# A fused retention and MLP kernel on one core: 64-token attention chunks and a rearranged lead-in

## The chip, the cores and the metric

The kernel runs on one core of a Trainium2 chip. The metric is the device time of one execution in microseconds (us), as a median over the fast runs. PE is the TensorE (matmul) engine, PEld its weight loads, DVE the VectorE, ACT the ScalarE, POOL the GpSimd engine, SP the SyncE. In this kernel POOL and SP issue the DMA transfers. Instants in a trace are us from the start of the profiled span, which is some 1.8 us shorter than the time reported for the run.

## The reference

It is a retention attention (causal, with one decay factor for each head) followed by an MLP with a sigmoid-approximated gelu.

```
# q, k, v: (8, 8, 576, 64) float32
scores = matmul(q, k.T) / sqrt(64)
D[h, i, j] = gamma[h] ** (i - j) if i >= j else 0
x = matmul(scores * D, v)            # to (8 * 576 = 4608, 512) tokens
h = x @ w_in                         # 512 x 2048
out = (h * sigmoid(1.702 * h)) @ w_out   # 2048 x 512, float32
```

## The kernel before

The 4,608 tokens are 36 units of 128 tokens; four units are a chunk of 512 tokens, and there are nine chunks, 0 to 8. For a chunk PE makes the up projection (16 groups of four 128x512 matmuls, each group followed by a gelu on ACT) and the down projection (four units of 16 matmuls). The attention of the next chunk's units is put into the down projection as two "blocks" of two units each. A unit needs its q, k and v loaded, q and k transposed (on PE for units 0 to 7, by DMA from unit 8 on), v scaled, scores, a running state of k and v for the tokens of earlier units, and the values.

The parts that the change touches, with cuts marked:

```
def lead_in():
    load_kq(0, 0); load_kq(0, 1)      # k and q of unit 0, POOL's (software) queue, cast to bf16
    load_v(0, eng="sp")
    load(1); load_win(0); load(2); load(3)
    for i in range(1, 4): load_win(i)
    for i in range(4): load_wout(i)
    for u in range(4, 10): load(u)    # ten units in all
    ...
def state(u):                         # 4 matmuls 128x128x128, of which half the result is used
    for hp in range(4): ... bank["K"] += k_pair.T @ v_pair
    ...                               # two casts on DVE to kv[u]
def block(j):                         # units 2j and 2j+1
    inter(2*j, 0); inter(2*j+1, 1)    # kv of the earlier units times q
    first = values_half(...)          # half of scores @ v
    scores(u, b) for the next two units
    values_half(..., phase 1)
    x_out_pair(...)
def steady():
    if c == 1:
        for u in range(10, 14): load(u, after=["T1_0"])      # wait for the transpose of unit 9
    for u in range(4*c + 6, 4*c + 10): dma_transpose(u)
    for u in range(4*c + 10, 4*c + 14): load(u, after=[transpose of unit 4*c + 9])
    ...                               # up groups, with state(m) after f = 2, 6, 10, 14
    ...                               # down groups, block after the first of units 0 and 2
```

`after=` makes a load wait for a DMA transpose. The names T0 to T7 are the eight buffers of transposed q and k; unit u uses T(u mod 8).

## Time and profile before

The kernel took 304.84 us (median of 3 runs, 304.63 to 305.48).

| what | us |
|---|---|
| first up group starts (timeline of PE) | 16.66 |
| down projection of chunk 0 starts | 35.76 |
| chunk 1 starts | 56.53 |
| chunk 1 takes | 31.68 |
| chunks 2 to 7 take | 183.95 |
| chunk 8, to PE's end | 27.83 |

The chain of waits of the same kernel around the change from chunk 0 to chunk 1, its longest pieces only (start, duration, engine, what, line; an x is a number of instructions):

```profile
52.05 1.73 PE psB L583 x8
...
54.29 0.76 DVE xT L550 x2
55.05 1.21 DVE pm L503 x2
...
56.60 0.76 PE psA L572 x4
...
74.33 2.54 PE psA L583 x11
76.86 3.45 PE psB L583 x16
```

Line 572 is the up projection, line 583 the down projection. In this stretch no DMA stands in the chain: the transposes of units 10 to 13 come in time.

A block as the timeline of PE shows it; the down group that is interrupted ends at about 195.6 and goes on at 196.9:

```profile
194.66 1.03 PE L583 MATMUL psA<-w_out_sb,gT 128*128 128x512 bf16 x4
195.62 0.24 PE L468 MATMUL psX<-kqT,kv 64*64 64x128 bf16 x1
...
196.89 2.54 PE L583 MATMUL psA<-w_out_sb,gT 128*128 128x512 bf16 x11 [0.16 <-issue]
```

### The profile page before, as it was taken

Reading aid. Unit: us, or ns where it says so; the run is one execution under the profiler, and the core shown is the slowest. Engines: PE = TensorE matmul, PEld = TensorE weight load, DVE = VectorE, ACT = ScalarE, POOL = GpSimd, SP = SyncE. Lnnn points to the kernel's source line nnn. Section 1 sums busy time; section 2 is a strip of 40 time slices with the busy share of each in tenths; the row PEclk is TensorE's granted clock in tenths of the full one; section 3 lists DMA queues with packets and bytes.
Section 4 is the critical chain, followed back from the end, with each engine's and each line's share of the span. In section 5 each row is a group of like instructions: output and inputs, shape, how many; then the busy total and the mean of one; then the engine's idle time right before and its main releaser. Section 6 shows DMA issues by size and latency. Waiting matters only on the chain.

```text
span 302.7 us, 6295 instructions
## 1 busy us (share of the span) xinstructions
PE 288.9 (95%) x2646; PEld 140.6 (46%) x2682; DVE 117.9 (39%) x246; ACT 126.4 (42%) x242; POOL 187.6 (62%) x276
## 2 busy tenths in 40 slices
PE   6599999999999999999999999999999999999996
PEld 2366355544544454444445444444444444543344
DVE  4759038655334433423443344234434443410000
ACT  6667534363136412641265126511651166117611
POOL 8999660699399959949982998399609600000000
PEclk9979999999999999999999999999999999999999
DMA  9999999999799979989997899699999840010022
GB/s 99 168 215 207 203 235 217 162 137 154 161 142 161 133 126 176 178 133 124 150 168 124 110 158 191 106 123 166 156 106 113 134 104 0 37 71 35 0 66 75
DMA packets 120396, 40.27 MB, mean 133 GB/s; under 512 B 109296, under 2 KB 113648, under 8 KB 120368
## 3 DMA queue, kind: packets, MB, share of 16 engines
q0 software_dynamic: 84368, 22.82, 70.9%
q1 hardware_dynamic: 36000, 17.05, 25.3%
q8 instruction: 21, 0.34, 0.5%
q14 instruction: 7, 0.06, 0.1%
HBM read 36.70 MB, written 9.44 MB: 152 GB/s over the span
## 4 chain that ended last, share of the span: by engine, by line
PE 91%; DMA 2%; POOL 2%; DVE 2%; issue 2%; POOLq 0%
PE psA L583 21%; PE psB L572 20%; PE psA L572 20%; PE psB L583 20%; DMA kqn<-in_q_dram 2%; PE psK L430 2%; PE psX L468 2%; POOL kqn L241 1%; PE psE L392 1%; PE psY L536 1%; DVE pm L503 1%; PE psX L536 1%; PE psD L495 1%; PE psB L495 1%; PE psC L484 1%
## 5 line engine op out<-in xcount | busy, mean ns | idle before, releaser
L241 POOL DMA_DIRECT2D kqn<-in_k_dram x94 | 68.0, 800 | 50.5 <-DMA kqT<-kqn 47.7
L572 PE MATMUL psA<-xT,w_in_sb 128*128 128x512 bf16 (+2 forms) x287 | 72.7, 371 | 0.9 <-ACT gT L577 0.3
L572 PE MATMUL psB<-xT,w_in_sb 128*128 128x512 bf16 (+2 forms) x289 | 72.3, 372 | 0.4
L259 POOL DMA_DIRECT2D vn<-in_v_dram x93 | 68.6, 845 | 1.1 <-issue 1.1
L583 PE MATMUL psA<-w_out_sb,gT 128*128 128x512 bf16 (+1 forms) x288 | 66.3, 373 | 2.3 <-issue 2.2
L583 PE MATMUL psB<-w_out_sb,gT 128*128 128x512 bf16 (+1 forms) x285 | 63.6, 373 | 0.3 <-issue 0.2
L241 POOL DMA_DIRECT2D kqn<-in_q_dram x70 | 56.6, 883 | 0.0
L577 ACT ACTIVATE gT<-psB 128x512 bf16<-128x512 f32 (+2 forms) x74 | 42.8, 579 | 24.8 <-PE psB L572 24.6
L442 DVE CAST kv<-psK 64x256 bf16<-64x256 f32 x56 | 23.6, 422 | 74.4 <-PE psK L430 73.8
L577 ACT ACTIVATE gT<-psA 128x512 bf16<-128x512 f32 (+2 forms) x74 | 42.7, 577 | 19.8 <-PE psA L572 19.7
L583 PEld LDWEIGHTS psA<-w_out_sb,gT 128*128 128x128 bf16 x304 | 28.2, 98 | 31.3 <-ACT gT L577 1.0
L583 PEld LDWEIGHTS psB<-w_out_sb,gT 128*128 128x128 bf16 x288 | 27.9, 98 | 31.8
L572 PEld LDWEIGHTS psA<-xT,w_in_sb 128*128 128x128 bf16 x296 | 25.7, 98 | 35.6 <-ACT gT L577 12.7
L572 PEld LDWEIGHTS psB<-xT,w_in_sb 128*128 128x128 bf16 x296 | 24.8, 98 | 29.5 <-ACT gT L577 10.5
L593 ACT ACTIVATE osb<-psA 128x512 f32<-128x512 f32 x18 | 10.7, 597 | 65.0 <-PE psA L583 65.0
L593 ACT ACTIVATE osb<-psB 128x512 f32<-128x512 f32 (+1 forms) x18 | 10.5, 586 | 46.7 <-PE psB L583 46.7
L511 DVE TENSOR_TENSOR pm<-psB,maskp 128x384 bf16<-128x384 f32 x12 | 6.7, 558 | 38.3 <-PE psB L495 38.3
L384 DVE TENSOR_TENSOR vp<-vn,vfac_s 128x512 bf16<-128x512 f32 x27 | 18.5, 690 | 1.9 <-DMA vn<-in_v_dram 1.4
L595 DVE COPY osb<-psA 128x256 f32<-128x256 f32 x1 | 0.4, 424 | 32.5 <-PE psA L583 32.5
L430 PE MATMUL psK<-vp,kqn 128*128 128x128 bf16 x128 | 12.7, 222 | 0.0
L430 PEld LDWEIGHTS psK<-vp,kqn 128*128 128x128 bf16 x128 | 9.5, 99 | 6.1
L402 ACT ACTIVATE kqT<-psE 128x512 bf16<-128x512 bf16 x14 | 7.7, 593 | 10.9 <-PE psE L392 10.9
(93 smaller groups left out, 229.7 us busy)
## 6 DMA issues: line engine op xcount, KB each, us to landing
out_dram<-osb SPq DMA_DIRECT2D x31, 256.0 KB, 2.7
vn<-in_v_dram POOLq DMA_DIRECT2D x60, 64.0 KB, 3.1
vn<-in_v_dram POOLq DMA_DIRECT2D x26, 128.0 KB, 3.7
kqn<-in_q_dram POOLq DMA_DIRECT2D x50, 64.0 KB, 3.7
w_in_sb<-in_moe_w_in_dram POOLq DMA_DIRECT2D x8, 256.0 KB, 8.5
w_out_sb<-in_moe_w_out_dram POOLq DMA_DIRECT2D x4, 512.0 KB, 15.5
kqn<-in_k_dram POOLq DMA_DIRECT2D x60, 32.0 KB, 3.0
vn<-in_v_dram POOLq DMA_DIRECT2D x7, 256.0 KB, 17.6
```

Source lines behind the costliest of these rows:

```text
L241: e.dma_start(kqn[sl][p0 : p0 + n, which, ds, :], src[b, ss, s0 : s0 + n, :].rearrange("h p d -> p h d"),)
L259: e.dma_start(vn[sl][p0 : p0 + n, ss, :], v[b, ss, s0 : s0 + n, :].rearrange("h p d -> p h d"),)
L384: op(eng, lambda e: e.tensor_tensor(vp[u % NVP].ap(), vn[sl].ap(), (vfac if u < NSW else vfac_s)[:, ty, :, None].to_broadcast([P, H, DH]), ...
L402: op("act", lambda e: e.activation(dst, src, AF.Copy), reads=[b], writes=[f"T{u % NQT}_{which}"])
L430: op("pe", lambda e, hp=hp: e.matmul(bank["K"][:, P * hp : P * hp + P], kq_pair(u, 0, hp), v_pair(u, hp), start=(c == 0 and hp == 0), stop ...
L442: op("dve", lambda e, dst=dst, src=src: e.tensor_copy(dst, src), reads=["K"], writes=[f"kv{u % NKV}_{hh}"])
L468: op("pe", lambda e, g=g, pb=pb, hh=hh, hp=hp, s=s, uv=uv, t0=t0, n=n: e.matmul(xbank(hh, slot)[64 * pb : 64 * pb + 64, g, t0 : t0 + n], k ...
L511: op("dve", lambda e: e.tensor_tensor(pm[u % 4][hh][:, 0:384].rearrange("p (a i) -> p a i", i=192), ps32(banks[hh])[:, 0:384].rearrange("p ...
L572: op("pe", lambda e, a=a: e.matmul(bank[b][:, n0:n1], w_in_sb[:, a, P * f : P * f + P], xT[c % 2][:, a, n0:n1], start=(a == 0), stop=(a == ...
L577: op("act", lambda e: e.activation(gT[c % 2][:, f, n0:n1], bank[b][:, n0:n1], AF.Gelu_apprx_sigmoid), reads=[b], writes=[f"g{c % 2}_{f}_{j ...
L583: op("pe", lambda e, f=f: e.matmul(bank[b][:, 0 : n1 - n0], gT[c % 2][:, f, P * r : P * r + P], w_out_sb[:, f, n0:n1], start=(f == 0), sto ...
L593: op("act", lambda e: e.activation(dst, src, AF.Copy), reads=[b], writes=[f"osb{i}_{n0}"])
```

## The change

The intent is to spend fewer array columns on attention by working in chunks of 64 tokens within a unit (fewer scores above the diagonal, no wasted half of the state), to start sooner, and to keep transfers out of each other's way. The diff, cut to its core:

```diff
 def lead_in():
-    load_kq(0, 0); load_kq(0, 1)
-    load_v(0, eng="sp")
+    load_kq0(0); load_kq0(1)          # float32, on SP's queue; DVE casts them
+    load_v(0)                         # on the software queue
     ...                               # w_in slices between units 1, 2, 3
-    for u in range(4, NPE + 2): load(u)
+    for u in range(4, NPE + 4): load(u)          # twelve units
-    warm(8) ...
+    warm(7) ... 31 filler matmuls of 512 columns in all, up groups of two and four f
@@ scores: 64 x 64 pieces only (before: 64 x 128, and from unit 9 on 64 x 128 and 64 x 64 mixed)
-    for hh in range(2): matmul(ps[:, P*hp : P*hp+P], ...)
+    for a in range(2):
+        for hh in range(2): matmul(ps[64*a : 64*a+64, 64 columns], ...)
@@ state: one 64x64 piece for each head and half instead of a full 128x128 product
-    matmul(bank["K"], k_pair, v_pair)  x4
+    matmul(ps32(KB[a])[64*hh : 64*hh+64, 64 columns], k half, v half)  x16
+    # state_sum: DVE adds to a float32 running sum; state_cast: ACT casts four at once
@@ block: the states move from the up phase into the block
+    ahead(j + 1)                      # scores and states of the next two units
@@ steady
     if c == 1:
-        for u in range(10, 14): load(u, after=["T1_0"])
+        dma_transpose(10); dma_transpose(11)
+        for u in (12, 13): load(u, after=["T3_0"])   # wait for the transpose of unit 11
+        ...                           # block(3) moved from chunk 0 to chunk 1
-    mask = [P, P], maskp, maskpc ... 
+    mask = [P, 2, 64]                 # keeps later DMA targets at multiples of 512 bytes
```

From then on the loads of units 14 to 17 wait for the transpose of unit 13, and so on, as before.

## The prediction

> **What bounds the kernel now.** The page puts PE at 95% busy and the chain of waits at PE 91%, nearly all of it the up and down projections. The timeline of PE gives one 128x512 matmul every 0.216 us, so a token chunk (128 of them) costs 27.6 us; chunks repeat every 30.7 us, and the 3.0 us between is attention: two blocks that stretch a down group by 1.16 and 1.06 us, and about 0.22 us for each state update between the up groups. No wait of PE on DMA stands in the steady part; DVE (39%) and ACT (42%) have room. The first 56.5 us hold only one chunk's projections (27.6 us); there PE follows the loads: the first up group starts at 16.6 us, behind the landing of unit 2's q (15.8 us), at a granted clock of 0.66 in the window 15 to 20 us, and the weight loads occupy the queue until about 37 us.
>
> **What the change does, costed.**
> 1. 64-token chunks. Per unit, in columns of one 64x64 quadrant: scores 384 to 256, values 384 to 256, history term 256 to 256 in twice the instructions, state 512 of the full array to 256. In the timeline, rounds of four 128-column quadrant matmuls step every 56 to 60 ns, rounds of 64 columns every 29 to 35 ns. [...] So twice the instructions do not eat the saving: a block plus its states goes from about 1.5 us to 32 rounds x 0.033 + 0.25 us of drain, 1.3 us. Over the six chunks after chunk 1, estimate: 18.2 us of attention become about 14.3. Gain 3.9 us, all on PE, hence critical.
> 2. State sums move to DVE (0.42 us each) and casts to ACT (about 1.0 us for 1,024 elements, estimated from 0.39 us at 256 and 0.60 at 512). Off the path unless the cast delays the eviction of bank A: I estimate it ends 5.8 to 6.4 us after the block, PE needs the bank at 6.3. Risk: 0.1 us a block.
> 3. First k and q as float32 on the SP queue, cast by DVE; V on the software queue; w_in interleaved; filler matmuls; grouped up projections; down groups 0 and 1 interleaved by weight slice. Expected: first up group near 13.5 us instead of 16.6, at full clock; down starts near 32 us instead of 35.8, then follows w_out and the loads of units 4 to 7; chunk 1 starts near 51.5 us instead of 56.5. Gain 5 us, the least certain term.
> 4. Chunk 1: two blocks cheaper, block 3 moved in: gain about 1 us. Loads 12 and 13 held back: neutral.
> 5. Alignment: by allocation both kernels already place every DMA target at a multiple of 512 bytes; gain 0. Fewer, full-partition loads halve POOL's issue time; POOL is not critical.
>
> Sum: 304.8 - 3.9 - 5 - 1 + 1 (step 2) = **296 us**, 8 in 10 between 291.5 and 300.5. Chances: faster by over 2% 0.78, within 2% 0.20, slower 0.02.
>
> **Would show it right:** PE step per round near 0.033 us; chunk period near 30.0 us; first up group by 14 us; POOL busy near 100 us; PE still above 94%. **Wrong:** PE waits on ACT osb or on DVE stm after blocks; period unchanged (rounds of 64 columns bound by issue); start of chunk 1 still near 55 us because w_out or the loads of units 4 to 7 land when they did before; waits of transposes 12, 13 in chunk 1.

The 0.033 us a round in the sum rest on the rounds of the timeline; 304.8 - 3.9 - 5 - 1 + 1 is 295.9, the 296 us of the forecast. The 0.25 us of drain are an estimate. In the timeline of the kernel before, 0.35 us pass from the start of a block's last small matmul to the start of the next 512-column one (196.54 to 196.89 us).

## More of the kernel before

The page of the profile gives busy times of the engines, then the busy share in 40 slices of 7.57 us (a digit 9 is 90% or more), the instruction queue among the DMA queues (packets, MB, share), and the chain of waits by engine:

```profile
PE 288.9 (95%) x2646; PEld 140.6 (46%) x2682; DVE 117.9 (39%) x246; ACT 126.4 (42%) x242; POOL 187.6 (62%) x276
...
PE   6599999999999999999999999999999999999996
...
q8 instruction: 21, 0.34, 0.5%
...
PE 91%; DMA 2%; POOL 2%; DVE 2%; issue 2%; POOLq 0%
```

PE is busy 95% of the span, and 91% of the chain that ended last is PE's. Apart from the last slice, where the kernel ends, PE is visibly short of work only in the first two. The line of queue 8 looks harmless: 21 packets in 300 us. It becomes important below; its packets are 0.34 MB / 21 = 16 KB each, and they are PE's own instructions (their number follows PE's instruction count, as shown below).

## The result

The changed kernel took 301.55 us (median of 4 runs, 300.90 to 302.38), against 304.89 us (304.63 to 305.48) for the kernel before on the same chip. The ratio is 0.9889, 95% interval 0.9855 to 0.9923: within 2%, where 296.0 us was predicted. Ratios here are the mean time of one kernel's fast runs over that of the other's fast runs of the same rounds, so not quite the ratio of the medians that are quoted. All results were correct except where it is said.

The same lines of the page, after:

```profile
PE 289.9 (97%) x3583; PEld 141.5 (47%) x3583; DVE 98.7 (33%) x198; ACT 135.1 (45%) x236; POOL 108.2 (36%) x137
...
PE   7989998989999999999999999999999999999996
...
q8 instruction: 28, 0.46, 0.7%
...
PE 67%; DMA 15%; POOL 14%; issue 2%; SPq 1%; ACT 0%; DVE 0%; POOLq 0%
```

PE is still "97% busy", but the chain that ended last is only 67% PE's. DMA and POOL have taken 29% of it. Busy shares alone would have hidden this. The share of a chain is not a loss of that size: of its DMA time 12.5 us are a later transpose (90.18 to 102.64 us), for which PE waited only 0.2 us. PE has 7,166 instructions (3,583 matmuls and as many weight loads) instead of 5,364 (2,682 weight loads and as many matmuls, of which the trace lacks 36), and fetches 28 blocks instead of 21. That is about 256 instructions to a block in both (7,166 / 28 = 255.9; 5,364 / 21 = 255.4).

The starts of the phases from the timeline of PE show where the time came from and went. The columns "control" and "fewer loads" are experiments told below: the same changed kernel once more, and the one in which 3.1 MB less are loaded.

| us | before | predicted | after | control | fewer loads |
|---|---|---|---|---|---|
| chunk 1 starts | 56.53 | 51.5 | 52.99 | 52.19 | 53.16 |
| chunk 1 takes | 31.68 | 30.7 | 34.18 | 37.61 | 32.11 |
| chunks 2 to 7 take | 183.95 | 180.05 | 181.47 | 180.60 | 180.55 |
| chunk 8 takes | 27.83 | 27.83 | 27.83 | 27.83 | 27.83 |
| PE ends | 299.99 | | 296.47 | 298.23 | 293.65 |

("Predicted" applies the gains that the prediction names to the column before.) The lead-in gained 3.5 us. Chunk 1 gave 2.5 us of it back, instead of gaining 1. The six chunks after it gained 2.5 us, instead of 3.9.

The chain of waits of the changed kernel in the same stretch as shown of before, again its longest pieces:

```profile
44.16 0.83 POOL kqn L214
44.99 18.05 DMA kqn<-in_q_dram
63.10 4.98 DMA kqT<-kqn
68.08 0.39 issue
68.48 1.76 POOL kqn L214 x2
70.23 0.89 POOL vn L227
71.12 0.82 POOL kqn L214
71.95 4.63 DMA kqn<-in_q_dram
76.64 3.80 DMA kqT<-kqn
80.48 0.21 PE psC L477
```

Where the kernel before had PE, this one has a relay of transfers. The last load of the lead-in takes 18 us to land, behind all the others. Then come the transposes of units 10 and 11 (5 us). Only then does POOL issue the loads of units 12 and 13. They land and are transposed (3.8 us), and PE's score matmuls (line 477) have been waiting for 0.7 us when the last transpose lands. The timeline of POOL shows the hold as one idle stretch (the bracket gives idle us and what ended it):

```profile
45.85 0.94 POOL L227 DMA_DIRECT2D vn<-in_v_dram  x1
68.48 0.88 POOL L214 DMA_DIRECT2D kqn<-in_k_dram  x1 [21.68 <-DMA kqT<-kqn]
```

The table by windows of the changed kernel shows that the DMA engines run nearly empty at the end of this hold. The last three columns are PE's granted clock, the DMA share (packets in flight at the same time are added up, so it can exceed 1) and GB/s:

```profile
40.00:56.00 16.00, 14.54 (x272) 8.69 (x271) 9.66 (x18) 8.96 (x16) 6.17 (x7) 1.00 1.90 226
...
66.00:70.00 4.00, 4.00 (x81) 3.38 (x81) 2.04 (x4) 2.46 (x5) 1.52 (x2) 1.00 0.16 33
```

From 226 GB/s the traffic falls to 33 GB/s. The kernel before moved 160 GB/s in the same 4 us:

```profile
66.00:70.00 4.00, 3.95 (x23) 1.78 (x22) 2.95 (x6) 2.39 (x4) 4.00 (x7) 1.00 1.04 160
```

Second, the timeline of PE has gaps that no semaphore ends; the profile calls them "issue". The two largest:

```profile
51.90 1.25 PE L562 MATMUL psB<-w_out_sb,gT 128*128 128x512 bf16 x5 [0.86 <-issue]
...
61.75 0.81 PE L550 MATMUL psB<-xT,w_in_sb 128*128 128x256 bf16 x6 [1.25 <-issue]
```

Line 562 is now the down projection and line 550 the grouped up projection. Both gaps lie in the middle of a group whose operands had long been there. A third such gap lies at 145.29 in the steady part. The kernel before has none of this size.

The part of the change that is in its name worked. The same place in a block after, one column of the timeline:

```profile
131.28 1.03 PE L562 MATMUL psA<-w_out_sb,gT 128*128 128x512 bf16 x4
133.44 2.76 PE L562 MATMUL psA<-w_out_sb,gT 128*128 128x512 bf16 x12
```

The block starts at 132.24 and the down group goes on at 133.44: 1.2 us for 128 matmuls of 64 columns, states included. Before, it was 1.27 us without the states. So the up phases, which had held the states, fell from 14.5 or 14.7 us to 13.81.

### The profile page after: what moved, and what is told of

Read it like the earlier page. It is cut to its first block, busy times and chain, and to the rows that moved or that the text cites. A ratio compares the mean times of both kernels' runs of the same rounds, so it can differ in the third digit from the quotient of the medians.

```text
span 299.2 us, 7913 instructions
## 1 busy us (share of the span) xinstructions
PE 289.9 (97%) x3583; PEld 141.5 (47%) x3583; DVE 98.7 (33%) x198; ACT 135.1 (45%) x236; POOL 108.2 (36%) x137
## 3 DMA queue, kind: packets, MB, share of 16 engines
HBM read 36.70 MB, written 9.44 MB: 154 GB/s over the span
## 4 chain that ended last, share of the span: by engine, by line
PE 67%; DMA 15%; POOL 14%; issue 2%; SPq 1%; ACT 0%; DVE 0%; POOLq 0%
PE psA L562 18%; PE psB L562 17%; PE psA L536 14%; PE psB L536 14%; DMA kqn<-in_q_dram 8%; POOL kqn L214 7%; DMA kqT<-kqn 7%; POOL vn L227 4%; POOL w_in_sb L252 2%; PE psX L461 1%; POOL w_out_sb L259 1%; PE psC L477 1%; PE psK L406 1%; PE psX L499 1%; SPq L371 1%
## 5 line engine op out<-in xcount | busy, mean ns | idle before, releaser
L214 POOL DMA_DIRECT2D kqn<-in_k_dram x39 | 35.0, 907 | 113.2 <-DMA kqT<-kqn 110.5
L536 PE MATMUL psA<-xT,w_in_sb 128*128 128x512 bf16 x232 | 59.5, 379 | 0.0
L536 PE MATMUL psB<-xT,w_in_sb 128*128 128x512 bf16 x232 | 59.5, 379 | 0.0
L430 ACT ACTIVATE kv<-stm 128x1024 bf16<-128x1024 f32 (+1 forms) x16 | 15.2, 949 | 71.9 <-DVE stm L421 71.9
L541 ACT ACTIVATE gT<-psA 128x512 bf16<-128x512 f32 x58 | 34.6, 597 | 15.5 <-PE psA L536 15.5
L541 ACT ACTIVATE gT<-psB 128x512 bf16<-128x512 f32 x58 | 34.6, 597 | 15.4 <-PE psB L536 15.4
L227 POOL DMA_DIRECT2D vn<-in_v_dram x40 | 36.9, 930 | 3.2 <-issue 3.1
L336 DVE TENSOR_TENSOR vp<-vn,vfac 128x512 bf16<-128x512 f32 x36 | 23.7, 687 | 43.4 <-DMA vn<-in_v_dram 43.4
L214 POOL DMA_DIRECT2D kqn<-in_q_dram x39 | 35.3, 917 | 0.0
L550 PE MATMUL psB<-xT,w_in_sb 128*128 128x256 bf16 (+1 forms) x128 | 14.7, 259 | 1.2 <-issue 1.2
```

Source lines behind the costliest of these rows:

```text
L214: e.dma_start(kqn[sl][p0 : p0 + n, which, :, :], src[b, :, s0 : s0 + n, :].rearrange("h p d -> p h d"),)
L227: e.dma_start(vn[sl][p0 : p0 + n, :, :], v[b, :, s0 : s0 + n, :].rearrange("h p d -> p h d"))
L336: op(eng, lambda e: e.tensor_tensor(vp[u % NVP].ap(), vn[sl].ap(), vfac[:, ty, :, None].to_broadcast([P, H, DH]), ALU.mult), reads=[f"vn{s ...
L430: op("act", lambda e: e.activation(kv[:, i0 % NKV : i0 % NKV + n, :, :], stm[:, i0 % 8 : i0 % 8 + n, :, :], AF.Copy), reads=[f"stm{(i0 + i ...
L536: op("pe", lambda e, a=a: e.matmul(bank[b][:, n0:n1], w_in_sb[:, a, P * f : P * f + P], xT[c % 2][:, a, n0:n1], start=(a == 0), stop=(a == ...
L541: op("act", lambda e: e.activation(gT[c % 2][:, f, n0:n1], bank[b][:, n0:n1], AF.Gelu_apprx_sigmoid), reads=[b], writes=[f"g{c % 2}_{f}_{j ...
```

## The experiments

### Theories

Theory F (refill): PE's instructions come in packets of 256 (28 for 7,166), on a queue that the page lists with those of the other transfers, and the next packet often lands only after PE has entered a block of 256. Where PE goes through 256 instructions faster than that packet takes to land, it stands still. The change made this likely: an attention block is 128 matmuls with 128 weight loads, so 256 instructions in about 1.2 us, where the kernel before took 8.1 us for its fastest 256. Up to 103 us in the first trace, the next packet landed 1.4 to 4.6 us after PE had entered a block of instructions, and once 7.7 us after (the block entered at 51.9 us, at a DMA share of 2.02 from 50 to 54 us). After 103 us packets land from 2.5 us before such an entry to 3.8 us after it. So the entry is not the moment at which a fetch begins, and these times are not those of the fetches themselves.

The supply theory: the loads of the lead-in, the transposes behind them and the hold form a chain of fixed length. PE can't be ahead of it, so what the lead-in gains is waited for at the transposes of units 12 and 13.

Rivals: the gaps belong to an operation or a time and not to the instruction count; the alignment of DMA targets matters; the lead-in's PE chain is the path, so that each us there counts.

### The changed kernel again, and its instruction blocks moved

The unchanged kernel ran again twice, each time on the chip of other experiments.

> The changed kernel unaltered, a second time, to see what repeats. Theory F (instruction refill): PE idles with nothing named ('issue') at three places of the first trace, 1.2, 1.5 and 0.9 us, all at the end of a stretch of 256 PE instructions counted from the same origin (index 1460, 1715, 4018 of the PE instructions, remainders 180, 179, 178 by 256). The same indices should stall again, between 0.5 and 1.6 us each, ratio to the kernel before 0.987 to 0.991. Rival D (data or DMA contention that happens to fall there): gaps of other sizes at other indices.

Measured: 300.75 us (300.24 to 302.75), ratio 0.987 (0.9837 to 0.9902). Two of the three gaps came again at the same indices, at 0.90 us and, smaller than expected, 0.42 us. The third did not come.

> The changed kernel once more, unchanged, on the chip of this batch, so that the other runs of the batch can be compared with it. Both theories: 300.1 to 302.4 us, ratio to the kernel before 0.986 to 0.990; gaps of PE near its instructions 1452 and 1715 (sizes 0 to 2 us), and a wait for the transposes of units 12 and 13 of 0.7 to 3 us in all.

Measured: 301.34 us (299.44 to 302.71), ratio 0.9878 (0.9849 to 0.9908). The result stands: 1.1 to 1.3% faster. Both profiles have waits for the transposes of units 12 and 13, of 3.0 and 2.0 us as gaps between PE's instructions. The single runs spread over 2.5 and 3.3 us, those of the kernel before over 2.4 and 1.4 us. Of the 16 runs of the changed kernel, the 11 at a granted clock of 1.0 have a mean of 300.9 us, the 5 at 0.994 one of 302.2 us; a stretch at half clock that makes such a difference is shown below.

Then the same work with more instructions in front: 31 or 13 of the filler matmuls of the lead-in were cut into four of 128 columns.

```diff
 def warm(n):
     for i in range(n):
+        if split[0]:                  # 31, or 13
+            split[0] -= 1
+            for j in range(4): matmul(bank["A"][:, P*j : P*j+P], gT[1][:, 0, 0:P], gT[1][:, 0, P*j : P*j+P])
+            continue
         matmul(bank["A"], gT[1][:, 0, 0:P], gT[1][:, 0, :])
```

> All 31 filler matmuls of 512 columns are cut into four of 128 columns each: the same array time, the same program otherwise, but 186 more PE instructions before the first real blocks, so the 256-instruction boundaries fall 186 instructions earlier in the program. Theory F: with a refill that takes 4.2 to 4.6 us from one boundary to being usable, replaying the trace's instruction times gives 0 to 0.3 us of stalls in place of 1.3 to 2.5 (3.0 measured): faster than the changed kernel by 2 to 3 us, about 298.5 to 299.5 us, no 'issue' gap over 0.5 us after the first 20 us. Rival D: same time as the changed kernel within 0.5 us, gaps at the same operations.

The 4.2 to 4.6 us of a refill are an estimate from the first trace, in which PE went on after its three gaps 4.3, 9.9 and 4.8 us after entering the block before (47.59 to 51.90, 51.90 to 61.75 and 140.49 to 145.29 us).

Measured: 304.47 us, ratio 0.9909 (0.9856 to 0.9962); two of six runs were slow, among them the profiled one, and the four fast ones took 300.67 to 304.85 us. The expectation of a gain was wrong. The gap in the steady part went, as expected. But the profiled run had two gaps of 3 and 4 us early on, where the page of this run has the DMA engines at 90% or more (209 and 149 GB/s in the slices of the two). As it is a slow run, only the places of its gaps are used here and not its times:

```profile
15.98 0.22 PE L500 MATMUL psX<-pm,vp 64*64 64x64 bf16 x2 [3.01 <-issue]
...
63.60 0.49 PE L551 MATMUL psB<-xT,w_in_sb 128*128 128x256 bf16 x3 [4.07 <-issue]
```

> The same with only 13 of the 31 fillers cut, 78 more instructions: the worst alignment that the replay finds. Theory F: stalls of 2.8, 1.5 and 1.2 us (at the first or second block of chunks 3, 4 and 5), in all 5 to 7 us instead of 1.3 to 2.5: 2.5 to 4.5 us slower than the changed kernel, 304 to 306 us, as slow as the kernel before. Rival D: same time as the changed kernel within 0.5 us.

Measured: 302.98 us (300.83 to 304.30), ratio 0.9918 (0.9884 to 0.9952), so 1.5 us slower than the unchanged kernel by ratio (0.9918 - 0.987 = 0.0048). The intervals of the two ratios overlap. New gaps of 0.67 and 0.84 us stood in the first block of chunk 3 and just after that of chunk 4, near where they had been expected. They were smaller than expected, and the third, in chunk 5, did not come. Something else in this trace matters below: chunk 1 took only 32.04 us, with no wait for a transpose, and then PE waited 1.85 us in chunk 2 for the transposes of units 14 and 15.

Counting PE's weight loads (3,583 in every trace of the same program, so no record of them seems to be missing) gives the position of each gap without a semaphore. Start of the gap in us, its length from start to start, and the number of weight loads so far, with the rest of a division by 128:

```
after            50.66 1.24  730 = 5*128+90    60.23 1.52  858 = 6*128+90   144.40 0.89 2009 = 15*128+89
once more        49.85 0.90  730               59.09 0.42  858
13 cut           48.59 1.09  730               132.41 0.67 1881 = 14*128+89  164.71 0.84 2265 = 17*128+89
31 cut           59.26 4.34  858
control          49.99 1.11  730               59.44 2.07  858
second block    117.79 2.82 1881              153.41 0.82 2521   176.76 0.46 2777   188.76 1.01 3161   (all rest 89)
```

Over all the traces there are 35 gaps over 0.4 us after the first 20 us that the profile puts down to "issue". All have a rest of 89 or 90, whatever instruction stands there: an up group, a down group, a block, a score. Of the few in the first 20 us one is large, that of the run with 31 cut, with a rest of 95. 128 weight loads with their matmuls are 256 instructions. So the gaps belong to the count and not to the operation, and the rival falls. That a gap does not come at every multiple fits: it needs a fetch that is late for its block.

The packets of queue 8 in the traces show this directly. At each of the 35 gaps PE goes on 1.2 to 2.6 us after the landing of the packet for the block that begins there: in the first trace the packets land at 50.66, 59.62 and 144.04 us, and PE goes on at 51.90, 61.75 and 145.29. After the first 20 us, no trace has PE entering a block less than 1.0 us after its packet.

### The second block

To see whether density alone makes such gaps, the scores of the next two units were computed four more times, 3.5 us after each block of chunks 2 to 7. In that stretch less is moved: 100 to 164 GB/s in the first trace's windows of 30 us from 90 to 240 us, against 209 from 12 to 40 us and 226 from 40 to 56 us.

```diff
+if c > 1 and s == 0 and r % 2 == 1:
+    j = 2 * c + 3 + r // 2
+    for u in (2 * j, 2 * j + 1) * 4:
+        if u < NU: scores(u)          # same values; nobody reads them
```

> The changed kernel with the suspected cost doubled, in the stretch where the loads leave the DMA engines room: 3.5 us after each block of chunks 2 to 7 the scores of the next two units are computed four times over (128 more 64-column matmuls, 256 PE instructions in about 1.06 us, same values, nobody reads them; 11 places). Refill theory: two dense stretches within 5.8 us ask for two blocks of instructions faster than the 1.4 to 4.6 us that a fetch takes there, so gaps of 0.5 to 3 us that no semaphore ends appear at four or more of the 11 places, and the cost is 15 to 30 us instead of the 11.7 us that the matmuls alone take. Rival (fetches keep up when the DMA engines are not full, the few gaps seen are something else): 11 to 13 us, no gap over 0.35 us.

Measured: 320.98 us (320.11 to 324.30), ratio 1.054 (1.0495 to 1.0585), about 20 us more than the control. The down phases without a gap show that 128 such matmuls cost 1.28 us each (chunk 7: 17.28 us instead of 16.00), more than the 1.06 us that the expectation had taken. Eleven of them are 14.1 us. The six down phases took 19.8 us more than the control's. The rest, 5.7 us, is gaps: four without a semaphore of 2.82, 0.82, 0.46 and 1.01 us at the counts listed above, and 0.67 us of waiting for a transpose. The largest of them in the timeline:

```profile
117.79 0.19 PE L477 MATMUL psD<-kqT 64*64 64x64 bf16 x1
120.61 0.21 PE L477 MATMUL psC<-kqT 64*64 64x64 bf16 x1 [2.63 <-issue]
```

It stands between two matmuls of one and the same group. Theory F is supported: with 128 more matmuls in 1.28 us some 3.5 us behind a block, PE stands still, here for 2.63 us, without waiting for any data. The page has 39 packets on queue 8 for PE's 9,982 instructions, again 256 to a packet. For the largest gap the packet landed at 119.07 us, 1.55 us before PE went on. Three of the four gaps are in the added matmuls and one just after them; the expectation of "four or more of the 11 places" was a little too high.

### The alignment of DMA targets

```diff
-mask = sb("mask", [P, 2, 64], BF16)
+mask = sb("mask", [P, 1, 64], BF16)   # all later DMA targets 128 bytes off
```

> The mask without its unused second half, so every tile behind it, DMA targets included, starts 128 bytes earlier: 384 instead of 0 modulo 512. The kernel before already had its targets at multiples of 512, so this tells what the padding keeps, not what it adds to the kernel before. If alignment matters to the transfers, the packets of the software queue take longer and the lead-in ends later (start of chunk 1 over 54 us instead of 53.0): 1 to 4 us slower. If not: the same within 0.7 us.

Measured: 301.22 us (300.06 to 302.38), ratio 0.9865 (0.9831 to 0.9899), against 0.987 for the unchanged kernel. The first up group came at 15.10 us instead of 13.88 in the profiled run, and chunk 1 started at 54.17 us, just past the 54 that the expectation had named as a sign. But chunk 1 then took only 32.25 us and the end did not come later (PE ends at 295.60 us, in the first trace at 296.47). The same late start stands in a run whose lead-in was not touched (below), so it is no sign of alignment. The alignment part of the change is worth nothing that these rounds can see. Both kernels have all their targets at multiples of 512 bytes by allocation anyway.

### The first loads as before

```diff
-load_kq0(0); load_kq0(1)
+load_kq(0, 0); load_kq(0, 1); load_v(0, eng="sp")
 ...
-load_v(0)
 ...
-cast_kq0(0, "dve"); cast_kq0(1, "dve")
```

> k and q of unit 0 are loaded as in the kernel before (converted on the software queue, v on the other queue) instead of as float32 with a cast on DVE. If the new way of loading unit 0 is what brought the first up group from 16.7 to 13.9 us: the first up group at 15.5 to 16.7 us. Theory of two limits (the weights and loads keep the DMA engines over 95% busy until 56 us, so what PE gains ahead of them is waited for later): of those 2 us or so, less than 0.7 us reach the end. Rival (PE's chain of the lead-in is the path): all 2 us reach the end, 302.5 to 304 us.

("Over 95% busy" is no figure of the tables, which add up packets in flight: in the first trace they give a DMA share of 1.51 from 12 to 40 us and of 1.90 from 40 to 56 us.)

Measured: 301.78 us (300.42 to 304.01), ratio 0.9893 (0.9856 to 0.9929), against 0.9878 for the control: no difference that can be told. In the traces the first up group is 1.44 us later than in the control (15.32 against 13.88), the down projection of chunk 0 2.05 us later and chunk 1 1.72 us later. Yet chunk 1's down projection starts at the same 69.97 us: in the control, the 1.7 us had been eaten by a gap of 2.07 us at the weight-load count 858. PE ends 0.65 us later. So in this pair of traces the head start is gone before chunk 1 is half done, and a third of it or a little more is seen at the end. This fits the theory of two limits better than "each us of the lead-in counts". But the pair proves little. The first up group also came at 15.20 us in the run with the states on DVE (below), whose lead-in is that of the changed kernel. What the new first loads gain is therefore not shown; that a late start need not reach the end, the trace of the alignment run shows as well.

### Without the hold

```diff
-load(u, after=["T3_0"])               # units 12 and 13
+load(u)
```

> The loads of units 12 and 13 follow those of unit 11 without a wait. Supply theory (the hold is on the path: it lets the DMA engines run nearly empty, share 0.16 to 0.18 between 66 and 70 us, and the transposes of units 12 and 13 then come 0.7 to 3 us late): the two loads land by about 70 us instead of 76.6, the wait for the transposes of units 12 and 13 goes away, the second chunk begins at 84.5 to 86 us instead of 87.1, and the end comes 1 to 2.5 us sooner than in the control. Rival (the intent of the hold: the two loads would take the bandwidth from the transposes of units 8 to 11 and from PE's instruction blocks): the transposes of units 10 and 11 land 3 to 5 us later than 68 us, the gap near instruction 1715 grows to 3 us or more, and the end is level with the control or later.

Measured: 308.21 us (305.71 to 309.95), ratio 1.0102 (1.0067 to 1.0137): 6.9 us slower than the control by the medians. My supply theory as stated for this run was wrong, and the rival was right. The waits of PE (us in all, times, the longest):

```profile
PE psC L477 <- DMA kqT<-kqn: 8.8, 3, 7.1
```

The same line of the control:

```profile
PE psC L477 <- DMA kqT<-kqn: 1.6, 2, 1.1
```

The two loads ran beside the transposes of units 10 and 11, and in the chain of waits these took 14.7 us instead of 5. They are needed at 71 us, before units 12 and 13. So the hold is not neutral, as I had predicted it to be. It is worth 7 us against no hold (a part of these is a halved clock, for 10.2 us of this trace, whose mean clock is 0.983). It also puts units 12 and 13 behind the transposes of units 10 and 11; whether another order avoids both waits is asked next.

### Other orders of the same loads

First, the hold of the kernel before: ten units in the lead-in, and units 10 to 13 behind the transpose of unit 9.

```diff
-for u in range(4, NPE + 4): load(u)
+for u in range(4, NPE + 2): load(u)
 ...
-dma_transpose(10); dma_transpose(11)
-for u in (12, 13): load(u, after=["T3_0"])
+for u in range(10, 14): load(u, after=["T1_0"])
```

> Only ten units are loaded in the lead-in, and the loads of units 10 to 13 wait for the transpose of unit 9, as in the kernel before; the transposes of units 10 to 13 follow them. Supply theory: there is one change-over between loads and transposes fewer; the transposes of units 8 and 9 land by 56 us, those of 12 and 13 by 78 us instead of 79.5 to 82, the 0.7 to 3 us of waiting for the latter shrinks to under 0.5, and the second chunk begins at 86 to 87.5 us instead of 87.1 to 89.8: 0.5 to 2 us faster than the changed kernel (ratio to before 0.981 to 0.986). Rival (the order is as good as any, the bandwidth of the first 80 us is what counts): a wait of the same size appears at another transpose (10 or 11, in the first block of chunk 1), and the time is level.

Measured: 302.22 us, ratio 0.9905 (0.9875 to 0.9935). No gain; the rival was right. The wait moved to the transposes of units 10 and 11, at 3.05 us between PE's instructions.

Second, the scores and states of units 12 and 13 twelve us later, in chunk 2, so that nothing in chunk 1 waits for their transposes:

```diff
-block(j)                              # j = 5 held ahead(6)
+block(j, lambda: None)
 ... chunk 2, after the second up group:
+ahead(6); ahead_out(6, False); cast_range(24, 4, "dve")
```

> The second block of chunk 1 no longer holds the scores and states of units 12 and 13; they are issued after the second up group of chunk 2, some 12 us later, with the cast of these states on DVE. Loads and holds as in the changed kernel. Theory (the wait for the transposes of units 12 and 13 is what takes the lead-in's gain back): no wait for them, the second chunk begins 0.7 to 3 us earlier (85.5 to 87 us), chunk 2 takes 0.6 us longer for the moved matmuls, and 0.5 to 2 us are left at the end (ratio to before 0.981 to 0.986). Rival: the transposes of units 14 to 17, whose loads follow those of 12 and 13, become the wait in chunk 2 (over 1 us), and the time is level.

Measured: 300.08 us (299.47 to 304.06), ratio 0.9844 (0.9812 to 0.9877). It looked like a gain of about 1 us, so it ran again:

> The kernel with the late scores of units 12 and 13 again, on the chip of this batch, to see whether it beats the changed kernel beyond its spread. If its gain is real: a ratio to the kernel before of 0.981 to 0.987, most runs between 299.4 and 300.5 us with a granted clock of 1.0; if not: 0.987 to 0.990.

Measured: 301.49 us (300.01 to 303.22), ratio 0.9882 (0.9853 to 0.9911). The gain was not reproduced. The traces suggest why: chunk 2 started at 85.99 and 84.04 us, against 87.1 to 89.8 us in the three traces of the changed kernel, but then PE waited 0.87 and 1.79 us in chunk 2 for the transposes of units 14 and 15, which are next in the relay, and the second trace had a refill gap of 1.26 us at weight load 2009. An early start of chunk 2 is not this order's alone: with the order of the changed kernel it came at 84.70 us in the run with 13 cut and at 86.42 in the alignment run.

> The two before together: hold as in the kernel before, and the scores of units 12 and 13 late. If both aim at the same wait, the sum of their gains does not appear: no better than the better of the two by more than 0.5 us. If the supply still limits elsewhere after either, the two add up: 2 to 3 us faster than the changed kernel, 298 to 299 us.

Measured: 303.70 us, ratio 0.9948 (0.993 to 0.9965). The two orders together are the worst of the three. The wait for units 10 and 11 was 3.7 us, and late scores can't help with that one.

Third, late scores and all loads two units further ahead. The first attempt was a mistake of mine. In program order the transposes of units 14 and 15 stood before the block of units 6 and 7, whose buffers they overwrite.

> The kernel with the late scores of units 12 and 13, and the loads moved ahead by two units: those of units 12 to 15 follow the transpose of unit 11, those of 16 to 19 the transpose of unit 15 and so on. Supply theory: the wait for the transposes of units 14 and 15 in chunk 2 (0.87 us in the profiled run of late scores) goes away, the rest as there: 299 to 300 us. Rival: the transposes of units 12 and 13 are delayed by the loads of 14 and 15 until after the late scores (about 91 us), and a new wait appears there.

Measured: a wrong result and 330.77 us, with PE waiting 30 us in chunk 1. It says nothing about the question. With these transposes behind that block:

```diff
-for u in (12, 13): load(u, after=["T3_0"])
+for u in range(12, 16): load(u, after=["T3_0"])
 ... after block(3), and at the start of each later chunk:
+for u in range(4*c + 8, 4*c + 12): dma_transpose(u)
+for u in range(4*c + 12, 4*c + 16): load(u, after=[transpose of unit 4*c + 11])
```

> Late scores of units 12 and 13 with the loads two units ahead, again; in the first attempt the transposes of units 14 and 15 stood in the program before the block of units 6 and 7, whose buffers they overwrite: wrong result, 30 us of waiting. Now they follow that block. Supply theory: no wait for the transposes of units 12, 13 (needed at 86 to 88 us) nor 14, 15 (needed at about 100 us, a wait of 0.9 and 1.8 us in the two profiles of late scores), the clock stays at 1.0: 297.5 to 300 us, ratio to before 0.977 to 0.983. Rival: the larger batch of loads delays the transposes of 12 and 13 until after 88 us, and the time is 300 us or more.

Measured: 301.49 us (298.85 to 303.57), ratio 0.9865 (0.9822 to 0.9908). The profiled run was slow and is not compared. One run was the fastest of any correct kernel here (298.85), but the median is level with the changed kernel. No version beat the changed kernel beyond its spread.

### Fewer bytes

If the load of the DMA engines causes both losses, then with fewer bytes both must go. Units 8 to 11 were not loaded; they use the data of units 0 to 3. The result is wrong, and 3.1 MB less are read (by the page, 33.55 MB from memory instead of 36.70). The first attempt had another mistake of order: the load of unit 16 stood before the scaling of v of unit 8, which read the same buffer.

> Wrong on purpose: units 8 to 11 are not loaded, they use the data of units 0 to 3, so 3.1 MB fewer are to be moved in the first 60 us; everything else as in the changed kernel. Supply theory (both the waits for transposes and the long instruction fetches come from DMA engines that are full until 56 to 62 us): the DMA engines are through by about 48 us, the gap near instruction 1452 shrinks from 0.6-2.5 to under 0.5 us, the one near 1715 goes, the transposes of units 12 and 13 land before 73 us, chunk 1 takes 31.5 to 32.5 us instead of 34 to 37, and the time is 297 to 299 us. Rival (the gaps come from PE's own instruction rate alone): the gap near 1452 stays at 0.6 us or more and the time falls by less than 1.5 us.

Measured: 320.03 us, PE waiting 20.5 us for that scaling. With the buffers given out without that conflict:

```diff
+def slot(u): return u - 8 if 8 <= u < 12 else u - 4 if 12 <= u < 16 else u % NLD
-for u in range(4, NPE + 4): load(u)
+for u in range(4, NPE): load(u)
```

> Wrong on purpose: the run without the loads of units 8 to 11 again (they use the data of units 0 to 3), with the buffers of later units given out so that no later load precedes a read of the earlier data; in the first attempt the load of unit 16 stood before the scaling of v of unit 8 in the program, and PE waited 20.5 us for it. What that attempt already showed stands: the gap near instruction 1452 was 0.49 us there, and none followed near 1707. Supply theory: the same two, the transposes of units 12 and 13 long landed when PE asks for them, chunk 1 at 31.5 to 32.5 us instead of 34 to 37, a granted clock of 1.0, 296.5 to 298.5 us. Rival (PE's own rate, not the DMA engines' load, sets chunk 1): chunk 1 still takes over 33.5 us and the time falls by less than 1.5 us.

Measured: 297.32 us (296.63 to 298.12), ratio 0.9738 (0.9702 to 0.9773), and as expected in every point. Chunk 1 took 32.11 us, the granted clock was 1.0, the gap near instruction 1452 was under 0.4 us and the one near 1707 had gone. PE waited for no transpose; the waits of PE begin with these, none of them in chunk 1 for q or k:

```profile
PE psA L565 <- issue: 2.4, 15, 0.2
PE psA L553 <- DMA w_in_sb<-in_moe_w_in_dram: 1.6, 2, 0.9
PE psA L652 <- DVE gT L677: 1.2, 1, 1.2
```

(The first line is 15 gaps of 0.16 us, one after each block. The other two belong to the lead-in.) The table by windows:

```profile
56.00:62.00 6.00, 5.79 (x111) 4.74 (x109) 3.69 (x6) 3.92 (x7) 3.07 (x4) 1.00 0.70 97
```

There PE was busy 5.79 us of 6, against 4.67 in the changed kernel:

```profile
56.00:62.00 6.00, 4.67 (x99) 3.64 (x98) 3.09 (x5) 3.25 (x6) 0.00 (x0) 1.00 1.42 107
```

So 3.1 MB of early loads cost about 4 us (301.3 or 301.5 against 297.3), and in these traces they cost it in chunk 1. Both kinds of transfer came sooner: the next instruction packet after PE's entry into the block at 51 to 52 us landed 2.5 us after that entry, against 7.7, 7.0 and 8.6 us in the three traces of the changed kernel. So the run does not separate the two losses. Nor is the place of the loss fixed: with all the loads, chunk 1 took 32.04 us in the run with 13 cut and 32.25 in the alignment run, but the one lost more in chunks 2 to 7 (183.82 us) and the other started chunk 1 later (54.17).

### A wait that cost more than its length

The control's wait for the transposes of units 12 and 13 ended at about 81.4 us. The table by windows of the control, with PE's granted clock third from the right:

```profile
80.00:82.00 2.00, 0.90 (x80) 0.79 (x80) 0.20 (x1) 0.00 (x0) 0.23 (x1) 1.00 1.16 362
82.00:84.00 2.00, 1.84 (x22) 0.77 (x11) 1.80 (x4) 0.00 (x0) 2.00 (x3) 0.69 0.42 34
84.00:86.00 2.00, 2.00 (x6) 0.69 (x5) 1.93 (x6) 0.00 (x0) 2.00 (x3) 0.50 1.75 128
86.00:88.00 2.00, 2.00 (x10) 0.93 (x9) 0.56 (x2) 1.54 (x2) 2.00 (x4) 0.96 1.66 191
```

After the wait the clock was halved for 3.4 us. Eight 512-column matmuls took 0.42 us each instead of 0.216, so 1.7 us more. The group in the timeline took 4.22 us for eleven matmuls, and the same group in the first repetition 2.54 us:

```profile
82.29 4.22 PE L562 MATMUL psA<-w_out_sb,gT 128*128 128x512 bf16 x11 [0.16 <-issue]
```

```profile
81.27 2.54 PE L562 MATMUL psA<-w_out_sb,gT 128*128 128x512 bf16 x11 [0.16 <-issue]
```

The first repetition had waited longer (gaps of 2.13 and 0.87 us) and kept its clock. So the loss is there in some runs and not in others. In the other fast traces a pair of gaps like this was followed by a halved clock twice (1.91 and 0.87 us with the first loads as before, 1.28 and 0.88 us with the states on DVE) and not followed by one twice (1.13 and 0.73 us with the second block, 0.77 and 0.86 us with the states on ACT). The kernel before has such a stretch too, in its lead-in: 3.41 us from 15.43 us. The tables by windows of the first loads as before, of the states on DVE and of the hold as before come to 3.4 us each. What decides whether a pair of gaps is followed by it was not shown. In the control it came after two gaps of 1.26 and 0.76 us with 16 small matmuls between them.

This accounts for chunk 1 of the control: 37.61 - 32.11 = 5.5 us more than with fewer loads, of which 2.0 us are the two gaps, 1.7 us the clock and 2.1 us the refill gap at count 858 (0.3 us too much in all, as the gaps are counted from start to start).

### States between the up groups

The last part looks at density from the other side. From unit 12 on, the 32 state matmuls of a pair of units leave the block and go between two up groups.

```diff
 def ahead(j): scores of both units
-    state_both(u) for both units
+    if j < 6: state_both(u) for both units
 ... chunks 2 to 8, after up groups 4 and 10:
+    states_up(2*c + 2 + (f == 10))    # matmuls, sums on DVE, cast on ACT
```

> From unit 12 on, the state matmuls of a pair of units (32 of the block's 128 matmuls) are issued between two up groups of the next chunk instead of within the block; the total of PE instructions is the same. Refill theory (a stall comes where PE goes through 256 instructions faster than the next 256 are fetched; a block of 256 in 1.0 us does it): a block now has 192 instructions and the fastest 256 take about 7 us, so no gap over 0.35 us that no semaphore ends after 90 us; the lead-in and chunk 1 stay as in the control; 0 to 1.2 us faster than the control and a narrower spread of times. Rival (the stall belongs to the position in the instruction stream, whatever the density): a gap of 0.4 to 0.9 us remains near instruction 4018 or at another multiple of 256, and the time is level. Against both: if the states cost more between up groups than in the block (a drain on either side, 0.1 us each), chunks take 0.2 us more and the end comes 1 us later.

(The 0.1 us for a drain is an estimate. In the first trace the step into the block at 132.24 us is 0.31 us instead of 0.216, and the step out of it, at 133.44 us, 0.13 us where the small matmuls before it are 0.01 us apart.)

Measured: 321.98 us, ratio 1.0555 (1.0528 to 1.0582). I expected up to 1.2 us of gain and got over 20 us of loss. PE waits for ACT:

```profile
PE psB L536 <- ACT gT L541: 16.3, 12, 1.7
```

In ACT's program the cast stands in front of the next gelus and waits for four sums on DVE. At 94.66 us, for one, ACT had been idle for 1.57 us until the last sum; the cast then took 1.06 us, and two gelus followed right behind it (95.62 and 96.10 us), for which PE's banks had waited. So I tried it with the cast on DVE:

```diff
-state_cast(2*j, 2*j + 2)              # ACT
+cast_range(..., "dve")
```

> The states from unit 12 on between up groups as in the run of that name which was 20.6 us slower, but with the cast of the states on DVE instead of ACT. There PE waited 16.3 us for ACT's gelu in 12 places; if the cause is that ACT[...] stood at the cast until the sums on DVE were done, these waits go away, the up phases take 13.8 + 0.6 to 0.9 us, the down phases 15.8 us, and the time is within 1.5 us of the changed kernel's. If the cause is the bank or the matmuls themselves, the up phases still take 17 to 18.5 us. Refill theory: no gap without a semaphore over 0.35 us after 90 us.

Measured: 303.31 us, ratio 0.9944 (0.9919 to 0.997). The wait for ACT is gone, so the cause was as described, though the time is 2 us above the changed kernel's, a little outside what was expected. The up phases take 14.65 or 14.78 us and the down phases 15.82, a period of about 30.55 us against 30.1 of the control: four units' states cost 0.9 us between up groups and 0.5 us within the blocks. There was no refill gap after 90 us, but the control had none there either, so the run tells nothing about theory F.

## Why the prediction was wrong

It said 296.0 us (291.5 to 300.5) and 0.78 for over 2% faster. The kernel came out at 301.55 us. By the first trace, the lead-in fell short of its gain by 1.5 us, chunk 1 by 3.5 us and chunks 2 to 7 by 1.4 us; less the 1 us that the sum had set aside for step 2, that is the 5.4 us missing. All five signs that were to show the prediction right came true or nearly so (a round near 0.032 us, a chunk period of 30.1 to 30.25 us, the first up group at 13.9 us, POOL busy 108 us instead of 100, PE at 97%). None of them looks at chunk 1. Step by step:

1. **64-token chunks, gain 3.9 us: the mechanism was right, and the size nearly.** A round of four 64-column matmuls took about 0.03 us (31 to 35 ns within a run of them in the first trace), and a block with its states 1.2 to 1.3 us. In the control's trace, which has no refill gap there, chunks 2 to 7 gained 3.35 us (183.95 - 180.60). The first trace gained 2.5 us, as it lost 0.9 us to a refill gap. The step asked only whether the array can issue that many instructions, and not whether PE can fetch them (28 packets instead of 21).
2. **Sums on DVE, casts on ACT, risk 1 us: did not occur** in the changed kernel, where PE's waits for ACT's evictions come to 0.3 us or less. The risk was real, as the 16.3 us show when the cast is moved to the wrong place. The 1 us was put into the sum as a cost and hid part of the error.
3. **Lead-in, gain 5 us: 3.5 to 4.7 us in the traces of the changed kernel** (chunk 1 at 51.85 to 52.99 instead of 51.5). The first up group came at 13.9 us, near the 13.5 predicted. The down projection started at 33.3 us in the first trace and 32.9 in the control, instead of 32. A refill gap of about 1 us at weight load 730 is in it.
4. **Chunk 1, gain 1 us: this step failed, and it decided the result.** Its time with two cheaper blocks was to be 30.7 us; it was 34.18 us in the first trace and 37.61 us in the control's, so it lost 2.5 and 5.9 us. Part of it was a plain error in the sum: block 3 and its extra drains came into chunk 1, and the run with fewer loads shows that without waits the chunk takes 32.11 us, 0.4 us more than before. So the gain of 1 us was not there to be had. The rest was missing from the prediction, which took PE to be the path here: waits for the transposes of units 12 and 13 (0.7, 2.0 and 3.0 us in three traces), the halved clock after them in some runs (1.7 us), and a refill gap at weight load 858 (0.4 to 2.1 us).
5. **"Loads 12 and 13 held back: neutral" was wrong.** The hold is worth 7 us against no hold. It also closes the chain (transposes of 10 and 11, then loads, then transposes of 12 and 13) for which PE waits. The prediction did list "waits of transposes 12, 13 in chunk 1" among the signs of being wrong; it saw the place, and gave it no cost.
6. **Alignment, gain 0: right**, within what five rounds can see.

Had chunk 1 gained its 1 us instead of losing 2.5, the kernel would have come out near 298.0 us, inside the range (an estimate: 301.5 - 3.5).

The prediction also read the lead-in as PE's chain with loads behind it. The table by windows had shown 206 and 224 GB/s from 12 to 40 and from 40 to 56 us in the kernel before; in the changed one it shows 209 and 226. So the earlier PE did not make these loads faster. It only met their end sooner: of the 3.5 us gained before 53 us, 2.5 were lost before 88 us. With 3.1 MB less to load the same kernel took 297.3 us. That this is close to the predicted number is luck and no confirmation: there chunk 1 started at 53.16 us and took 32.11, each over 1.4 us more than predicted.

What stays open: the share of the two losses (late transposes and late instruction packets), which were both smaller with 3.1 MB less to load, and an order of the loads that avoids both. None of the five tried did. The six transposes from 45 to 85 us landed 2.7 to 6.1 us after their issue in the kernel before, 3.8 to 11.3 us in the changed one, 2.8 to 15.1 us without the hold, and 2.7 to 6.4 us with 3.1 MB less to load. That the packets are late because the loads fill the DMA engines is not shown by itself: it rests on their landing times and on the run with fewer loads, and no run changes only the fetches. Open too is why the loss falls in chunk 1 in some traces and elsewhere in others.

## What to carry to other kernels

When a change starts an engine sooner, follow the transfers that feed it further on and ask whether they come sooner as well; where they do not, as here, the gain can be lost in waiting for a later tile. Let the signs that would show a prediction right cover every term of its sum. Cutting matmuls into small ones costs instructions, not only issue time (here 7,166 instead of 5,364): count the instructions in the densest stretch, and compare the time that PE takes for 256 of them (here 1.2 us) with the landing time of the 16 KB packets of the instruction queue, above all while much is being loaded (here 7.0 to 8.6 us after the entry at 51 to 52 us, and 2.5 us with 3.1 MB less). Read the chain of waits beside the busy share: PE was 95% and 97% busy in two kernels whose chains were 91% and 67% PE's. Then read from the gaps of the engine what a piece of the chain really costs.
